# Routing search of a mixture of experts: four guessed rounds, the rest in a conditional on VectorE

## Chip, cores and metric

The kernel runs on one NeuronCore of a Trainium2 chip. The metric is the device time of one execution in microseconds; 630.14 us is the median of three runs before the change.

## What is computed

Attention with a sliding window, then a mixture of experts whose tokens are assigned greedily. In short:

```python
# q, k, v: (8, 8, 576, 64); window 64
x = softmax_window(q @ k.T / 8) @ v          # as 4608 tokens x 512
logits = x @ w_gate                          # 4608 x 8
cap = 4608 // 8                              # 576 tokens an expert
for idx in argsort(-logits.flatten()):       # best pair first
    tok, e = divmod(idx, 8)
    if assigned[tok] < 0 and counts[e] < cap:
        assigned[tok] = e; counts[e] += 1
out[mask_e] = relu(x[mask_e] @ w1[e]) @ w2[e]   # w1: 512x1024, w2: 1024x512
```

The greedy order needs no sort. Whichever expert fills first has the highest threshold: the score of its 576th token. The kernel finds that expert and its threshold, gives away all pairs above it, takes the expert out, and repeats for the next. Experts are numbered here in the order in which they fill, 0 to 7.

## The kernel before

The attention takes the first quarter of the time. It also leaves the scores in SBUF, as 128 partitions x 36 columns x 8 experts. Then two things run together for each of the eight experts: routing (finding the expert, its threshold and the list of its tokens) and the products.

**The search** (`search`) finds the threshold of an expert in eight rounds of four bits. A round compares each token's best score with 15 thresholds (`compare`, line 586, VectorE), counts the hits of every expert with nine matmuls (line 632, TensorE; the one-hot tile `one4` is the weight), and some thirteen short VectorE instructions find the highest threshold at which any expert is still full (lines 641 to 694). The next round's thresholds depend on it. Expert 0 is searched otherwise (`first`): three rounds in steps of the mean top score `mu`, and a conditional (line 765) with `search` as its block, on TensorE and VectorE, which is skipped when the three rounds have decided. Expert 7 takes what is left.

**Behind the search** come, in `steps`: the expert's number `ei` (line 946), which the loads of its weights read; its mark on every token, `X`; a scan (829); two matmuls for positions (832, 833); the listing of its 576 tokens (`listing`; 18 matmuls on 921, eight on 933, the index tile `idx` on 939); and the bookkeeping for the next search. Then `turn` gathers the tokens (line 1103, five indirect DMAs from GpSimd) and transposes them on TensorE (1141).

**The products** (`Experts.steps`): layer one is 160 matmuls (line 1203) over eight groups of 128 hidden units, layer two 112 (1237 and 1247). Every operand is split into a high and a low half in a faster float format. Weights come in chunks of 512 KB: SyncE loads `st`, ScalarE copies it to the high half and its negative to the low half, and a DMA from GpSimd adds `st` (line 1046) once the expert's gathers are issued. Eight chunks fit, which is one expert. VectorE subtracts low halves of the activations in layer one (1164, 1172) and adds once early in layer two (1224).

**Order.** The instructions of every engine are issued in an order fixed when the program is built. `Streams` is a small planner: generators yield the time that they think a step takes, and are resumed in order of planned time. So TensorE's queue holds products with the matmuls of search rounds, positions, lists and transposes put in at planned places, and waits in order at each. `yield lambda: ...` holds a generator until the condition is true in the plan; `self.dve(dt)` and `self.busy(dt)` book planned time on an engine. `ex.first` counts the layers one that are issued. In the kernel before, routing of the next expert starts as soon as that of the one before is finished, wherever the products are.

The loop that drives it:

```python
def route():
    for p in range(E):
        for dt in rt.steps(p):
            if p in rt.eint and p not in known and (p or rt.T is not None):
                known.add(p)
                st.add(ex.load(p, rt.eint[p]))
            yield dt
```

Of the kernel before, what the change touches and what calls it, by code (L numbers as in the profile page):

```python
# [10 lines left out]
FT = mybir.dt.float32  # L11
# [12 lines left out]
E = 8  # L24
# [415 lines left out]
BRANCH = [mybir.EngineType.PE, mybir.EngineType.DVE]  # L440
SLACK = (0, 0) + (100,) * 6
# [3 lines left out]
class Routing:  # L445
# [39 lines left out]
    def constants(self, jp, t):  # L485
# [20 lines left out]

        diag = t("diag", [128, 4])
# [70 lines left out]
    def mean_out(self):  # L578

        nc = self.nc  # L580
        nc.vector.tensor_scalar(self.mu, self.total, 1.0 / (128 * HEAD), None, op0=OP.mult)
        return [lambda: nc.vector.tensor_scalar(self.thr0, self.thr0, self.mu, None, op0=OP.mult)] + [lambda j=j: self.compare(self.G0, self.thr0, j, j + 4) for j in range(0, LATE, 4)]
# [25 lines left out]
    def search(self, p, code, one4, copied=0):  # L608

        nc, tile_ = self.nc, self.wk.tile  # L610
        slack = SLACK[p]
# [4 lines left out]
        for r in range(NR):  # L616
            G = tile_([128, NJ, ND], BF, name="G")
            c4 = self.room(128, 72)
            cn, c4 = c4[:, 64:72], c4[:, 0:4 * ND]
            for j0, j1 in ((0, 20), (20, 36)):  # L620
                self.compare(G, thr, j0, j1)
                yield self.dve(480 - 4 * j0)
            for f in rest:
                f()
            if r:
                self.dve(360, 2)
            yield max(slack, copied - self.clock() if not r else 0)
            kept, self.kept = self.kept, None
            if kept is not None:
                nc.tensor.matmul(cn, self.ones, kept, start=True, stop=True)  # L630
            for j in range(0, NJ, 4):
                nc.tensor.matmul(c4, one4[:, j // 4].rearrange("p k e -> p (k e)"),  # L632
                                 G[:, j:j + 4].rearrange("p j d -> p (j d)"),
                                 start=(j == 0), stop=(j == NJ - 4))
            self.joined()
            yield self.busy(350) + 200 + slack
            if kept is not None:
                nc.vector.tensor_tensor(self.left, self.left, cn, OP.add)

            dg = tile_([128, 4, ND], FT, name="dg")  # L640
            nc.vector.tensor_tensor(dg, c4.rearrange("p (k d) -> p k d", k=4),
                                    self.diag[:, :, None].to_broadcast([128, 4, ND]), OP.mult)
            sq = self.sq[r % 2]
            nc.vector.tensor_reduce(sq[:, 0:ND], dg.rearrange("p k d -> p d k"), axis=AX.X, op=OP.add)
            yield self.dve(530, 2) + (150 if kept is not None else 0)
            st = self.st
            nc.vector.transpose(st[:, 0:4].rearrange("p k e -> p (k e)"), sq)
            cnt = tile_([128, E], FT, name="cnt")
            nc.vector.tensor_reduce(cnt, st.rearrange("d k e -> d e k"), axis=AX.X, op=OP.add)
            yield self.dve(490, 2)  # L650

            step = float(1 << 28 - 4 * r) if r else 1.0
            pq = self.pq[r % 2]
            nc.vector.tensor_scalar(pq[:, 0:E], cnt, 0.0, step, op0=OP.is_ge, op1=OP.mult)
            pt = tile_([128, 32], FT, name="pt")
            nc.vector.transpose(pt, pq)
            yield self.dve(440, 2)
            ps = tile_([128, 1], FT, name="ps")
            nc.vector.tensor_reduce(ps, pt[:, 0:ND], axis=AX.X, op=OP.add)
            num = tile_([128, 32], FT, name="num")  # L660
# [61 lines left out]
    def first(self, code, X, run):  # L722
# [42 lines left out]
        with self.tc.If(go != 1):  # L765
# [3 lines left out]
            for _ in self.search(0, code, one4):  # L769
                pass  # L770
# [579 lines left out]
```

## Time and profile before

| | |
|---|---|
| three runs | 628.88, 630.14, 632.12 us |
| profiled execution | 627.58 us |
| its span, first to last instruction | 625.9 us |
| mean granted TensorE clock | 0.987 |
| TensorE busy | 598.2 us, 96% |
| VectorE busy | 457.8 us, 73% |
| ScalarE busy | 371.7 us, 59% |
| GpSimd busy | 187.2 us, 30% |

The profiled execution is a run of its own, with its own time beside its span; rows and stretches of the profile belong to it, not to the median. A busy share is the union of the times in which an engine had an instruction of the program in work. TensorE's matmuls are pipelined and overlap, so what one costs is read from the distance between starts, not from its duration.

### The profile page before, as it was taken

How to read it: one execution, taken by the hardware profiler on the slowest of the kernel's cores; microseconds unless marked ns; L12 is line 12 of the kernel's file. 1: busy time of each engine (PE TensorE's matmuls, PEld its weight loads, DVE VectorE, ACT ScalarE, POOL GpSimd, SP SyncE). 2: the span in 40 equal slices, each digit the busy share in tenths (PEclk: the TensorE clock that was granted, in tenths of full speed). 3: DMA queues.
4: the chain of work that ended last, by engine and by line, in shares of the span. 5: the costliest groups of instructions: out<-in, count | busy, mean ns of one | idle time of the engine just before them, and what ended most of it. 6: DMA issues, size and time to landing. Idle time of an engine off the chain costs nothing.

```text
span 625.9 us, 16201 instructions
## 1 busy us (share of the span) xinstructions
PE 598.2 (96%) x5966; PEld 509.8 (81%) x5966; DVE 457.8 (73%) x2151; ACT 371.7 (59%) x798; POOL 187.2 (30%) x245
## 2 busy tenths in 40 slices
PE   8999999996499999999999999999999999999996
PEld 6677778785399789888988988898889779888984
DVE  7888888887789779869977996898788717604400
ACT  6799889995474386267445837565564637515310
POOL 1324454440331261053126205321620560011011
PEclk9999999998699999999999999999999999999999
DMA  8999999951597599199659918975974798110001
GB/s 311 356 360 367 367 392 366 338 210 70 179 249 154 179 248 250 22 315 248 120 183 245 246 43 286 242 137 208 210 204 102 261 248 296 63 42 35 2 25 50
DMA packets 44944, 128.81 MB, mean 206 GB/s; under 512 B 4672, under 2 KB 5312, under 8 KB 44864
## 3 DMA queue, kind: packets, MB, share of 16 engines
q1 hardware_dynamic: 30592, 79.00, 35.2%
q0 software_dynamic: 13984, 48.25, 33.2%
q8 instruction: 47, 0.77, 0.5%
q10 hardware_dynamic: 288, 0.52, 0.3%
q14 instruction: 33, 0.27, 0.1%
HBM read 82.14 MB, written 18.87 MB: 161 GB/s over the span
## 4 chain that ended last, share of the span: by engine, by line
PE 53%; issue 17%; POOL 2%; DMA 1%; DVE 1%; ACT 1%; POOLq 0%; ACTq 0%
PE h L1203 24%; PE o L1247 20%; PE o L1237 3%; PE rps L632 2%; PE tp L1141 2%; POOL out L1226 2%; DMA xg<-xs,idx 1%; PE rps L593 1%; PE rps L921 1%; DMA xs<-x 0%; ACT R L905 0%; PE rps L923 0%; POOLq L1346 0%; DVE hl L1172 0%; PE rps L933 0%
## 5 line engine op out<-in xcount | busy, mean ns | idle before, releaser
L1203 PE MATMUL h<-xh,wh 128*128 128x320 f32 (+2 forms) x800 | 161.6, 333 | 0.0
L1203 PEld LDWEIGHTS h<-xh,wh 128*128 128x128 f32 x800 | 124.6, 188 | 5.2 <-ACT xh L1091 0.2
L1226 POOL DMA_INDIRECT out<-ot,idx x40 | 41.1, 1028 | 224.0 <-DVE ot L1224 79.6
L1247 PE MATMUL o<-wh,hl 128*128 128x512 f32 x256 | 101.0, 395 | 0.0
L1247 PE MATMUL o<-wl,hh 128*128 128x512 f32 x256 | 100.8, 394 | 0.0
L1247 PE MATMUL o<-wh,hh 128*128 128x512 f32 x256 | 100.7, 393 | 0.0
L141 ACT ACTIVATE pe<-st,mx 128x128 f32<-128x128 f32 x288 | 91.9, 393 | 5.7 <-DVE mx L136 5.5
L1203 PE MATMUL h<-xh,wl 128*128 128x256 f32 (+1 forms) x512 | 91.2, 297 | 0.0
L1203 PEld LDWEIGHTS h<-xh,wl 128*128 128x128 f32 x512 | 78.8, 188 | 4.4
L1030 ACT ACTIVATE wh<-st 128x1024 fp32r<-128x1024 f32 x64 | 67.3, 1051 | 2.8 <-DMA st<-w 2.8
L136 DVE CUSTOM_DVE_ANT_0 st<-Sp,mask 128x128 f32<-128x128 f32 x288 | 63.8, 285 | 6.7 <-PE Sp L128 5.7
L1217 ACT ACTIVATE ot<-o 128x512 f32<-128x512 f32 x32 | 19.1, 598 | 81.9 <-PE o L1247 81.8
L1046 POOL DMA_DIRECT2D wl<-st x51 | 46.5, 972 | 63.2 <-ACT wl L1044 34.2
L1247 PEld LDWEIGHTS o<-wh,hh 128*128 128x128 f32 x256 | 48.1, 188 | 9.5
L1247 PEld LDWEIGHTS o<-wl,hh 128*128 128x128 f32 x256 | 48.1, 188 | 9.4
L1247 PEld LDWEIGHTS o<-wh,hl 128*128 128x128 f32 x256 | 48.1, 188 | 9.3
L1044 ACT ACTIVATE wl<-wh 128x1024 fp32r<-128x1024 f32 x51 | 53.9, 1057 | 0.7
L1164 DVE TENSOR_TENSOR sum<-h,sum 128x256 f32<-128x256 f32 x56 | 23.2, 414 | 38.6 <-ACT sum L1162 38.4
L1167 ACT ACTIVATE hh<-h 128x320 fp32r<-128x320 f32 (+1 forms) x72 | 31.0, 431 | 31.1 <-PE h L1203 30.3
L150 ACT ACTIVATE pt<-Tp 128x512 f32<-128x512 f32 x72 | 42.1, 587 | 7.2 <-PE Tp L148 7.0
L1103 POOL DMA_INDIRECT xg<-xs,idx x32 | 31.2, 976 | 48.2 <-DVE eq L845 39.8
L176 PE MATMUL Op<-VO,pt 128*64 128x73 f32 x608 | 43.0, 230 | 1.0 <-issue 0.5
(210 smaller groups left out, 1100.4 us busy)
## 6 DMA issues: line engine op xcount, KB each, us to landing
st<-w SPq DMA_DIRECT2D x59, 512.0 KB, 7.3
wl<-st POOLq DMA_DIRECT2D x51, 512.0 KB, 6.4
xs<-x SPq DMA_DIRECT2D x36, 256.0 KB, 4.7
VO<-v SPq DMA_DIRECT2D x6, 1168.0 KB, 17.9
Q<-q SPq DMA_DIRECT2D x6, 1152.0 KB, 13.5
K<-k SPq DMA_DIRECT2D x6, 1152.0 KB, 16.1
VT<-vt SPq DMA_DIRECT2D x6, 1152.0 KB, 16.4
st<-w POOLq DMA_DIRECT2D x5, 512.0 KB, 7.5
```

What stands on the lines that cost most here:

```text
L136: nc.vector.tensor_tensor_reduce(st[:, h, :], Sp[h % 2][:, h // 2], mk, scale=-0.125, scalar=3.0e38, op0=OP.add, op1=OP.min, accum_out=mx[ ...
L141: nc.scalar.activation(pe[:, h, :], st[:, h, :], AF.Exp, bias=mx[:, h:h + 1], scale=-1.0)
L150: return pt, lambda: nc.scalar.activation(pt.rearrange("p h q -> p (h q)"), Tp, AF.Copy)
L176: nc.tensor.matmul(Op[g][64 * a:64 * a + 64, h, :], pt[:, h, 64 * a:64 * a + 64], vv[a][:, 4 * g + h, :], start=True, stop=True)
L1030: nc.scalar.activation(hi, st[i], AF.Copy)
L1044: nc.scalar.activation(lo, hi.bitcast(FT), AF.Copy, scale=-1.0)
L1046: nc.gpsimd.dma_start(lo.bitcast(FT), st[i], accum_op=OP.add)
L1103: nc.gpsimd.indirect_dma_start(out=g[a][0:n], out_offset=None, in_=self.xs, in_offset=IndirectOffsetOnAxis(ap=idx[0:n, a:a + 1], axis=0))
L1167: nc.scalar.activation(hh[:, f, c0:c1], h, AF.Relu)
L1203: nc.tensor.matmul(h[:, 0:w], wv[:, cc, 128 * (f % 2):128 * (f % 2) + 128], x[:, cc, x0:x0 + w], start=(k == 0), stop=(k == 4 * len(terms) ...
L1226: nc.gpsimd.indirect_dma_start(out=self.out[5 * p + a], out_offset=IndirectOffsetOnAxis(ap=idx[0:m, a:a + 1], axis=0), in_=ot[0:m], in_off ...
L1247: nc.tensor.matmul(o, ht[:, f, 128 * a:128 * a + 128], wt[:, 512 * (f % 2):512 * (f % 2) + 512], start=(k == 0), stop=(k == 23))
```

## The change

For experts 1 to 6 the search of eight rounds gives way to `guessed`: four rounds, with 15 thresholds each, that start from the threshold `T` of the preceding expert and cover the stretch from `T - 1.25 mu` to `T`; each round divides a sixteenth of the one before, the last in fifteen steps. The thresholds are floats from a table `gtab`, made in the setup by four instructions and scaled by `mu` once. The last round also counts whether one token more would fit, and writes into `go` the number of experts that fill there, or 0 if the step holds more than one token.

Then the stream is held until layer one of the preceding expert is issued (`opened`) and 700 planned ns more. A conditional on VectorE alone follows: if `go` is not 1, its block makes the whole search of eight rounds, with the counting done by VectorE products and sums (`alone`) in place of matmuls. The plan books 6000 + 300 ns for it. The number, the loads, the list and the gathers follow as before.

`search` is cut into `tally` (its old lines from the allocation of `c4` to `cnt`, moved as they are, and left out below), `alone` and `highest` (its old lines from `step` to `num`). Expert 0's search keeps its form; both conditionals now have the block named as not the preferred way on (`preferred_fallthrough_block=False`), and the plan's clocks are restored after the block.

```diff
 GUESS = 22
 LATE = 20
 BRANCH = [mybir.EngineType.PE, mybir.EngineType.DVE]
+ALONE = [mybir.EngineType.DVE]
+NG = 4
+WIDE = 1.25
 SLACK = (0, 0) + (100,) * 6
 U32 = mybir.dt.uint32
 
...
+        steps = t("gtab", [128, NG, ND])
+        for r in range(NG):
+            f, o = (WIDE / 16 ** (r + 1), 0.0) if r < NG - 1 else (WIDE / (ND * 16 ** r), -WIDE / (ND * 16 ** r))
+            yield nc.vector.tensor_scalar(steps[:, r], dgf, f, o, op0=OP.mult, op1=OP.add)
...
-    def search(self, p, code, one4, copied=0):
+    def tally(self, G, one4, r, rest, copied, slack):
...
+    def alone(self, G, r, rest):
+
+        nc, tile_ = self.nc, self.wk.tile
+        for f in rest:
+            f()
+        if not r:
+            self.P = tile_([128, E, 32], FT, name="P", bufs=1)
+            self.four = tile_([128, 5, E], FT, name="four", bufs=1)
+            nc.vector.memset(self.P, 0.0)
+            nc.vector.tensor_copy(self.four[:, 4], self.left)
+        P, four = self.P, self.four
+        Pt = tile_([128, E, 32], FT, name="Pt", bufs=1)
+        for e in range(0, E, 2):
+            H = tile_([128, NJ // 4, 4, 4 * E], BF, name="one4").rearrange("p q k e -> p (q k e)")
+            H = H[:, 0:2 * NJ * ND].rearrange("p (e j d) -> p e j d", e=2, d=ND)
+            nc.vector.tensor_tensor(H, G[:, None].to_broadcast([128, 2, NJ, ND]),
+                                    self.one[:, :, e:e + 2].rearrange("p j e -> p e j")[:, :, :, None]
+                                    .to_broadcast([128, 2, NJ, ND]), OP.mult)
+            nc.vector.tensor_reduce(P[:, e:e + 2, 0:ND], H.rearrange("p e j d -> p e d j"), axis=AX.X, op=OP.add)
+        nc.vector.transpose(Pt.rearrange("p e d -> p (e d)"), P.rearrange("p e d -> p (e d)"))
+        nc.vector.tensor_reduce(four[:, 0], Pt, axis=AX.X, op=OP.add)
+        for q in range(1, 4):
+            nc.vector.tensor_copy(four[0:32, q], four[32 * q:32 * q + 32, 0])
+        cnt = tile_([128, E], FT, name="cnt")
+        nc.vector.tensor_reduce(cnt[0:32], four[0:32].rearrange("d k e -> d e k"), axis=AX.X, op=OP.add)
+        for q in range(1, 4):
+            nc.vector.tensor_copy(cnt[32 * q:32 * q + 32], cnt[0:32])
+        yield 0
+        return cnt
+
+    def highest(self, cnt, r, step, n=1):
+
+        nc, tile_ = self.nc, self.wk.tile
+        pq = self.pq[r % 2]
+        for i in range(n):
+            nc.vector.tensor_scalar(pq[:, E * i:E * i + E], cnt, float(i), step, op0=OP.is_ge, op1=OP.mult)
+        pt = tile_([128, 32], FT, name="pt")
+        nc.vector.transpose(pt, pq)
+        yield self.dve(330 + 110 * n, 1 + n)
+        ps = tile_([128, 1], FT, name="ps")
+        nc.vector.tensor_reduce(ps, pt[:, 0:ND], axis=AX.X, op=OP.add)
+        num = tile_([128, 32], FT, name="num")
+        nc.vector.transpose(num, ps.to_broadcast([128, 32]))
+        yield self.dve(430, 2)
+        return num[:, 0:E * n]
+
+    def search(self, p, code, T, one4=None):
...
+            self.compare(G, thr, 0, NJ)
+            cnt = yield from self.alone(G, r, rest) if one4 is None else self.tally(G, one4, r, rest, 0, 0)
+            num = yield from self.highest(cnt, r, float(1 << 28 - 4 * r) if r else 1.0)
...
-                b2 = self.Tb if not p and r == NR - 1 else tile_([128, 1], I32, name="base")
+                b2 = T.bitcast(I32) if r == NR - 1 else tile_([128, 1], I32, name="base")
...
+    def guessed(self, p, code, one4, copied):
+
+        nc, tile_ = self.nc, self.wk.tile
+        tab, slack = self.gtab, SLACK[p]
+        if p == 1:
+            nc.vector.tensor_scalar(tab, tab, self.mu, None, op0=OP.mult)
+        base = tile_([128, 1], FT, name="base")
+        nc.vector.scalar_tensor_tensor(base, self.mu, -WIDE, self.T, op0=OP.mult, op1=OP.add)
+        thr = tile_([128, ND], FT, name="thr")
+        nc.vector.tensor_scalar(thr, tab[:, 0], base, None, op0=OP.add)
+        self.dve(450, 2)
+        rest = []
+        for r in range(NG):
+            G = tile_([128, NJ, ND], BF, name="G")
+            for j0, j1 in ((0, 20), (20, 36)):
+                self.compare(G, thr, j0, j1)
+                yield self.dve(480 - 4 * j0)
+            cnt = yield from self.tally(G, one4, r, rest, copied, slack)
+            if r == NG - 1:
+                break
+            num = yield from self.highest(cnt, r, tab[:, r, 0:1])
+            d = tile_([128, 1], FT, name="d")
+            nc.vector.tensor_reduce(d, num, axis=AX.X, op=OP.max)
+            thr = tile_([128, ND], FT, name="thr")
+            nc.vector.scalar_tensor_tensor(thr, tab[:, r + 1], d, base.to_broadcast([128, ND]), op0=OP.add, op1=OP.add)
+            b2 = tile_([128, 1], FT, name="base")
+
+            def rebase(b2=b2, base=base, d=d):
+                nc.vector.tensor_tensor(b2, base, d, OP.add)
+
+            rest = [rebase]
+            base = b2
+            yield self.dve(450, 2)
+        num = yield from self.highest(cnt, r, 1.0, 2)
+        d = tile_([128, 2], FT, name="d0", bufs=1)
+        nc.vector.tensor_reduce(d, num.rearrange("p (k e) -> p k e", k=2), axis=AX.X, op=OP.max)
+        q8 = tile_([128, E], FT, name="q8")
+        nc.vector.scalar_tensor_tensor(q8, num[:, 0:E], d[:, 0:1], self.all8, op0=OP.is_equal, op1=OP.mult,
+                                       accum_out=self.num1)
+        nc.vector.scalar_tensor_tensor(self.go, d[:, 0:1], d[:, 1:2], self.num1, op0=OP.is_gt, op1=OP.mult)
+        T = tile_([128, 1], FT, name="T")
+        oh = tile_([128, ND], FT, name="oh0", bufs=1)
+        nc.vector.scalar_tensor_tensor(oh, self.dgf, d[:, 0:1], thr, op0=OP.is_equal, op1=OP.mult, accum_out=T)
+        self.number(q8, code)
+        yield self.dve(1100, 5)
+        yield lambda: self.opened(p)
+        yield 700
+        go = nc.values_load(self.go[0:1, 0:1], engines=ALONE, min_val=0, max_val=E)
+        ends = dict(self.ends)
+        with self.tc.If(go != 1, preferred_fallthrough_block=False):
+            for _ in self.search(p, code, T):
+                pass
+        self.ends.clear()
+        self.ends.update(ends)
+        self.T = T
+        yield self.dve(6000) + 300
 
...
         go = nc.values_load(self.go[0:1, 0:1], engines=BRANCH, min_val=0, max_val=E)
         ends = dict(self.ends)
-        with self.tc.If(go != 1):
+        with self.tc.If(go != 1, preferred_fallthrough_block=False):
             one4 = tile_([128, NJ // 4, 4, 4 * E], BF, name="one4")
             nc.vector.tensor_copy(one4, one.rearrange("p (q k) e -> p q (k e)", k=4)[:, :, None, :]
                                   .to_broadcast([128, NJ // 4, 4, 4 * E]))
-            for _ in self.search(0, code, one4):
+            self.T = self.Tb.bitcast(FT)
+            for _ in self.search(0, code, self.T, one4):
                 pass
             self.marked(self.T, code, X, run)
+        self.ends.clear()
         self.ends.update(ends)
-        self.T = self.Tb.bitcast(FT)
         yield 0
 
     def steps(self, p):
@@ -794,7 +893,7 @@
                     nc.scalar.copy(one4[:, j0:j1], one1[:, j0:j1, None, :].to_broadcast([128, 3, 4, 4 * E]))
                 copied = self.clock() + self.busy(1260, "act") + 200
             if p:
-                yield from self.search(p, code, one4, copied)
+                yield from self.guessed(p, code, one4, copied)
             else:
                 run = tile_([128, 2 * NJ], BF, name="run")
                 self.expert(p, code, False)
@@ -1326,6 +1425,7 @@
             st.add(ex.turn(p, idx))
 
         known = set()
+        rt.opened = lambda p: ex.first >= p
         rt.listed, rt.spawn, rt.clock, rt.ends = listed, st.add, ex.clock, st.end
         st.add(route())
         st.add(products())
```

## Rows read from the trace of the kernel before

**Rows 1.** The page, part 1: busy time, share of the span, instructions.

```profile
PE 598.2 (96%) x5966; PEld 509.8 (81%) x5966; DVE 457.8 (73%) x2151; ACT 371.7 (59%) x798; POOL 187.2 (30%) x245
```

**Rows 2.** Waits of TensorE, 170 to 550 us: total, times, longest in us.

```profile
PE rps L921 <- POOL R L897: 0.8, 1, 0.8
PE tp L1141 <- DVE xh L1095: 0.3, 1, 0.3
```

**Rows 3.** TensorE's busy time, clock and DMA in a layer one.

```profile
231.00:258.00 27.00, 27.00 (x213) 1.00 0.78 176
```

**Rows 4.** Timeline of TensorE, early in layer two of expert 1.

```profile
260.01 0.39 PE L1237 MATMUL o<-wh,hh 128*128 128x512 f32 x1
...
260.82 0.39 PE L1237 MATMUL o<-wh,hh 128*128 128x512 f32 x1
```

**Rows 5.** Lines 1203, 1237 and 632 by windows: experts 1, 4, 6.

```profile
L1203 PE MATMUL h<-xh,wh x96: 302/309/482, 230.4 to 257.4; 128*128 128x320 f32 x64, 128*128 128x512 f32 x32
...
L1237 PE MATMUL o<-wh,hh x8: 388/389/393, 258.2 to 261.7; 128*128 128x512 f32 x8
...
L1203 PE MATMUL h<-xh,wh x96: 302/309/482, 401.3 to 427.6; 128*128 128x320 f32 x64, 128*128 128x512 f32 x32
...
L1237 PE MATMUL o<-wh,hh x6: 389/391/397, 428.4 to 430.8; 128*128 128x512 f32 x6
...
L632 PE MATMUL rps<-G,one x54: 188/191/202, 399.0 to 422.9; 128*128 128x60 bf16 x54
...
L1203 PE MATMUL h<-xh,wh x96: 302/309/398, 515.9 to 540.4; 128*128 128x320 f32 x64, 128*128 128x512 f32 x32
...
L1237 PE MATMUL o<-wh,hh x5: 389/393/397, 541.1 to 543.7; 128*128 128x512 f32 x5
```

**Rows 6.** Timeline of VectorE and TensorE at expert 0's conditional.

```profile
158.11 0.31 DVE L720 TENSOR_TENSOR_SCAN run<-X 128x72 bf16<-128x72 bf16 x1
...
159.41 0.22 PE L832 MATMUL h<-X,tri 128*128 128x72 bf16 x1 [3.09 <-DVEq L765]
```

**Rows 7.** Timeline of VectorE, from the end of expert 1's layer one.

```profile
259.18 0.21 DVE L1172 SCALAR_TENSOR_TENSOR hh<-h,hh 128x64 fp32r<-128x64 f32 x1
...
263.01 0.68 DVE L1224 TENSOR_TENSOR ot<-o,low 64x512 f32<-64x512 f32 x1 [0.19 <-ACT low L1221]
...
264.14 0.14 DVE L946 TENSOR_SCALAR ei<-code 1x1 int32<-1x1 f32 x1
...
265.48 0.31 DVE L829 TENSOR_TENSOR_SCAN run<-X 128x72 bf16<-128x72 bf16 x1
```

**Rows 8.** The chain that ended last: start us, us, what.

```profile
200.94 0.93 PE o L1237 x4
201.87 0.27 PE rps L632 x9
...
210.99 0.05 PE rps L832
...
215.27 0.54 PE rps L921 x18
...
485.36 3.20 PE o L1237 x14
488.55 0.54 PE rps L921 x18
```

**Rows 9.** Line 1141, 200 to 232 us: idle before it, times.

```profile
  DMA xg<-xs,idx: 0.5, 2
```

**Rows 10.** Line 1046, 223 to 223.5 us: ns, start, time to landing.

```profile
L1046 POOL DMA_DIRECT2D wl<-st x1: 1021/1021/1021, 223.2 to 223.2; - x1
...
DMA to landing us min/median/max: 5.5/5.5/5.5
```

**Rows 11.** The page, part 6: KB each, median us to landing.

```profile
st<-w SPq DMA_DIRECT2D x59, 512.0 KB, 7.3
```

**Rows 12.** Groups of VectorE, 204 to 262 us: busy us, mean ns, idle.

```profile
L908 DVE TENSOR_TENSOR B<-r,sb 128x1152 bf16<-128x1152 bf16 x1 | 1.3, 1266 | 0.0
```

More of the change, by code (lines that the diff above doesn't have):

```diff
@@ L606, in dve @@
         return self.busy(dt - 110 * n, "dve") + 110 * n
-    def search(self, p, code, one4, copied=0):
+    def tally(self, G, one4, r, rest, copied, slack):
         nc, tile_ = self.nc, self.wk.tile
-        slack = SLACK[p]
+        c4 = self.room(128, 72)
+        cn, c4 = c4[:, 64:72], c4[:, 0:4 * ND]
+        for f in rest:
+            f()
+        if r:
+            self.dve(360, 2)
+        yield max(slack, copied - self.clock() if not r else 0)
+        kept, self.kept = self.kept, None
+        if kept is not None:
+            nc.tensor.matmul(cn, self.ones, kept, start=True, stop=True)
+        for j in range(0, NJ, 4):
+            nc.tensor.matmul(c4, one4[:, j // 4].rearrange("p k e -> p (k e)"),
+                             G[:, j:j + 4].rearrange("p j d -> p (j d)"),
+                             start=(j == 0), stop=(j == NJ - 4))
+        self.joined()
+        yield self.busy(350) + 200 + slack
+        if kept is not None:
+            nc.vector.tensor_tensor(self.left, self.left, cn, OP.add)
+        dg = tile_([128, 4, ND], FT, name="dg")
+        nc.vector.tensor_tensor(dg, c4.rearrange("p (k d) -> p k d", k=4),
+                                self.diag[:, :, None].to_broadcast([128, 4, ND]), OP.mult)
+        sq = self.sq[r % 2]
+        nc.vector.tensor_reduce(sq[:, 0:ND], dg.rearrange("p k d -> p d k"), axis=AX.X, op=OP.add)
+        yield self.dve(530, 2) + (150 if kept is not None else 0)
+        st = self.st
+        nc.vector.transpose(st[:, 0:4].rearrange("p k e -> p (k e)"), sq)
+        cnt = tile_([128, E], FT, name="cnt")
+        nc.vector.tensor_reduce(cnt, st.rearrange("d k e -> d e k"), axis=AX.X, op=OP.add)
+        yield self.dve(490, 2)
+        return cnt
@@ new lines, in alone @@
+    def alone(self, G, r, rest):
+        nc, tile_ = self.nc, self.wk.tile
+        for f in rest:
+            f()
+        if not r:
[16 more added lines that the diff above has]
+            nc.vector.tensor_copy(four[0:32, q], four[32 * q:32 * q + 32, 0])
+        cnt = tile_([128, E], FT, name="cnt")
+        nc.vector.tensor_reduce(cnt[0:32], four[0:32].rearrange("d k e -> d e k"), axis=AX.X, op=OP.add)
+        for q in range(1, 4):
+            nc.vector.tensor_copy(cnt[32 * q:32 * q + 32], cnt[0:32])
+        yield 0
+        return cnt
@@ L617, in search @@
             G = tile_([128, NJ, ND], BF, name="G")
[L618 to L659, printed above, removed]
@@ L691, in search, with first @@
             q2 = tile_([128, E], FT, name="q8")
-            def highest(q2=q2, num=num, d=d, q8=q8):
+            def first(q2=q2, num=num, d=d, q8=q8):
                 nc.vector.scalar_tensor_tensor(q2, num, d[:, 0:1], q8, op0=OP.is_equal, op1=OP.mult)
-            rest.append(highest)
+            rest.append(first)
             q8 = q2
-            yield self.dve(450, 2) if r else self.dve(700, 3)
         for f in rest:
             f()
-        yield self.dve(450, 2)
-        self.T = base.bitcast(FT)
@@ L703, in search @@
         self.number(q8, code)
+    def guessed(self, p, code, one4, copied):
+        nc, tile_ = self.nc, self.wk.tile
+        tab, slack = self.gtab, SLACK[p]
[49 more added lines that the diff above has]
+        yield self.dve(6000) + 300
```

6 lines of the change are left out of this document (1 added, 5 removed).

## Prediction

> **What bounds the kernel now.** I read the page's share of each engine first: TensorE is busy 96% of the span [rows 1]. A busy TensorE can still hide waits, so the next view is what its matmuls waited for from 170 us, where the first expert's products begin, to 550 us: two waits, 1.1 us in all, neither of them in a search [rows 2]. The reader is to see that nothing holds TensorE there. Its clock doesn't either: in a layer one with search rounds the granted clock is 1.00, the 2.4 GHz level, and TensorE busy for all of 27 us [rows 3]. So the experts are one queue of matmuls, and what a search costs is the place of its own matmuls in that queue. By the program there are eight rounds of nine counting matmuls (line 632) for each of experts 1 to 6: 48 rounds, 432 matmuls. A microsecond of them taken out is a microsecond off the end, as long as what replaces them comes in time.
>
> **What a round costs TensorE.** There are three readings. The chain gives a round 0.27 us, from the first of its matmuls to the next product's [rows 8]. The timeline gives more: from 260.01 to 260.82 stand two products of layer two and a round, and products alone follow each other in 0.23 us (four in 0.93 us, rows 8), so the round is 0.81 - 0.46 = 0.35 us [rows 4]; the product behind it is late as well. Whole layers give the third: layer one of expert 4 begins at 401.3 and layer two at 428.4, 27.1 us, with five rounds inside (six in the window, the first at 399.0 ahead of the layer); that of expert 6, with none, runs from 515.9 to 541.1, 25.2 us [rows 5]; 1.9 / 5 = 0.38 us. I take the middle one, 0.35, which is read directly and with all that belongs to the round; the ends are 0.27 and 0.38.
>
> **What the change removes.** Four of eight rounds for six experts: 24 rounds, 24 x 0.35 = 8.4 us of TensorE (6.5 to 9.1). Four rounds of VectorE work leave each layer one too, over a dozen short instructions each. Since TensorE waits for none of it now [rows 2], that gives nothing.
>
> **What it adds.** (a) Four table instructions in the setup. Short VectorE instructions take 0.14 to 0.21 us [rows 7], so between 0, if they fall into gaps of the attention, and 0.8 us; between such ends I take 0.4. (b) The guessed rounds do what the old ones did, in floating point for bits: nothing. The last has one more comparison and five short instructions after it, some 1.2 us at 0.2 each; then the stream waits for layer two, about a third of a layer later, and this hides it. Without that wait the listing would come 1.2 us later.
>
> (c) Six conditionals on VectorE. The trace has one, that of expert 0, and its skip can be read: VectorE's last instruction before it ends at 158.42, and TensorE's first matmul behind it, released by line 765, starts at 159.41 [rows 6]. So a skip is at most 0.99 us, the hand-over to TensorE included. The new ones are issued 0.7 us into layer two. For expert 2, layer two of expert 1 begins at 258.2 [rows 5]; VectorE's last instruction for layer one ends at 259.39 and its next duty to the products, the addition on line 1224, starts at 263.01 [rows 7]. The skip stands between, with 3.6 us of cover: nothing. Behind it on VectorE wait that addition and the expert's number, X and scan, and for these the position matmuls. The program puts those 0.7 + 6.3 + 0.78 + 0.65 + 0.44 = 8.9 us into layer two (its own planned steps). From the number's start, 264.14, to the scan's end, 265.79, VectorE needs 1.65 us, the addition 0.7. With 1.2 us until VectorE is free, a skip up to 8.9 - 1.2 - 0.7 - 1.65 = 5.3 us (a hand-over included) holds up nothing; every microsecond beyond is TensorE's, six times.
>
> (d) The moved step. An expert's number, weights, listing and gathers now begin in layer two of the preceding expert, however early the search ended. This passes SyncE's queue (the loads read the number) and GpSimd's (five gathers, then the low halves of the weights). The listing's matmuls came 4.3 us behind the position matmuls (210.99 to 215.27), so they will stand 13.2 us into layer two. Before, that was 14.3 us for expert 1 (200.94 to 215.27) and had drifted to 3.2 us for expert 6 (485.36 to 488.55) [rows 8]. So expert 1 gains a microsecond, expert 6 loses ten, and expert 1's rows show what the late place costs: its transposes waited 0.5 us for gathered rows [rows 9], and its first low half, issued behind the gathers at 223.2, landed 5.5 us later at 228.7 [rows 10], while layer one began at 230.4 [rows 5] and wants it after four products, at 231.3. That left 2.6 us. The new place is 1.1 us earlier and layer two shorter by two rounds, 0.7 us, so about 3 us are left. The cost is 0 to 0.5 us each for experts 2 to 6; I take 0.2, in all 1.0 us, being nearer to hidden. If the cover were gone, each microsecond of delay would be TensorE's.
>
> (e) Expert 0's block goes out of the straight path. By rows 6 this can save up to 0.99 us; if the new path is worse it can lose as much: 0.
>
> A rule speaks against (c). The Trainium skill (Runtime: NRT & Kernel Launch, section Instruction fetch mechanics) says that instructions stream in sequentially and that a taken branch to a place not yet loaded stalls for a fetch. The one skip of this trace took 0.99 us at most [rows 6], so here it shows no stall as long as a transfer of rows 11. What a stall would make of the time is the second rival below.
>
> **The sum.** -8.4 + 0.4 + 1.0 = -7.0 us. The profiled execution took 627.58 us (span 625.9), so the changed one would show 620.6. The median of the runs, 630.14, is 2.56 above the profiled one: 623.1 us is the forecast.
>
> **The rivals.** *Late weights or rows.* The late place bites harder than it did for expert 1. If the first low half takes 4 us more than the 5.5 us of rows 10, the 3 us are used up and layer one waits 1 us, in six experts 6 us: 623.1 + 6 = 629.1 us. For it: later experts' transfers share the queues with the preceding expert's stores, and a weight load from memory takes 7.3 us in the median [rows 11]. Against: TensorE waited for no weights at expert 1's place [rows 2].
>
> *The skip is long* (slower). VectorE has to fetch the code it jumps to, and does nothing until it is there. No row times that. The ends are nothing beyond the 0.99 us of rows 6 and a whole weight load, 7.3 us [rows 11]; then a skip is 8.3 us, 3.0 over the 5.3, and six cost 18 us: 641 us. The gain is gone where a skip takes 5.3 + 7.0 / 6 = 6.5 us. For it: the new blocks hold eight rounds of over twenty-five instructions, more than expert 0's. Against: rows 6, the nearest in kind.
>
> *The guess misses*, its block runs, and the change doesn't do what it says. On VectorE alone a round counts by four products over 1080 elements and four sums of as many; at the 1.27 us of the row with 1152 elements [rows 12] that is at least 8 x 1.2 = 9.6 us, eight rounds 77 us, nearly all in the open: about 700 us for one miss. Against: worked out from the reference's inputs, each of the six thresholds lies 0.002 to 0.84 mean scores under the one before (the window is 1.25), and the next score is 0.0005 or more below, against a finest step of 0.00002.
>
> **How the numbers follow.** The forecast case gets 0.78, late weights 0.12 (0.05 of it, with half the delay, still faster by over 0.5%), the long skip 0.08, a miss 0.02. A measurement of this kernel tells about 0.5%, 3.2 us, from no change; its three runs lie 3.2 us apart. So faster 0.83, same 0.07, slower 0.10. Low end: rounds at 9.1, expert 0's skip at 0.99 and the two additions at nothing give 620.0; with a microsecond for the spread of runs, 619.0. High end: the smallest saving, 6.5, with 0.8 and 2.5 added gives 626.9; 627.5 takes in the near part of the late weights.
>
> **What would show it.** The counting matmuls should number 216 instead of 432. Layer one of expert 4 should take some 26.4 us instead of 27.1 (three rounds inside instead of five), the period of an expert 1.4 us less. Position matmuls should stand about 8.9 us into layer two, listing 13.2, with no wait of TensorE in front. VectorE should show a hole of about a microsecond early in layer two and none of the block's work. The forecast is wrong if that hole passes 5.3 us, if a layer one begins with a wait for weights or transposes, or if a layer one doesn't shrink by 0.35 us for each round it lost.

## The result and the profile after

Four runs of the changed kernel took 619.33 to 622.03 us, median 620.21; four of the kernel before 628.88 to 632.12, median 630.78. The ratio is 0.984 (95% interval 0.980 to 0.987): faster by 10.6 us where 7.0 were forecast, and inside the range. The two profiled executions, 627.58 and 619.33 us, differ by 8.25.

The page of the changed kernel, its first part, answers to [rows 1]: VectorE lost 60 us of work and 319 instructions, TensorE 216 instructions, the counting matmuls of 24 rounds, as said.

```profile
PE 591.4 (96%) x5750; PEld 505.6 (82%) x5750; DVE 397.6 (64%) x1832; ACT 372.8 (60%) x798; POOL 186.2 (30%) x245
```

What TensorE waited for from 165 to 550 us (total, times, longest in us) answers to [rows 2]. The wait for the listing (0.8 us) is gone. The first row is new: four times TensorE now waits for VectorE's comparisons ahead of a counting round.

```profile
PE rps L629 <- DVE G L593: 1.3, 4, 0.3
PE tp L1240 <- issue: 0.5, 1, 0.5
PE tp L1240 <- DVE xh L1194: 0.2, 1, 0.2
PE h L1302 <- DVE xh L1194: 0.2, 1, 0.2
```

Layers one and two of experts 4 and 6, by windows of lines 1302, 1336 and 629 (xcount: duration min/median/max in ns, first and last start in us), answer to [rows 5].

```profile
L1302 PE MATMUL h<-xh,wh x96: 303/309/483, 394.4 to 421.1; 128*128 128x320 f32 x64, 128*128 128x512 f32 x32
...
L1336 PE MATMUL o<-wh,hh x8: 389/389/398, 421.9 to 425.1; 128*128 128x512 f32 x8
...
L629 PE MATMUL rps<-G,one x27: 188/191/202, 395.5 to 406.9; 128*128 128x60 bf16 x27
...
L1302 PE MATMUL h<-xh,wh x96: 302/309/471, 507.0 to 532.0; 128*128 128x320 f32 x64, 128*128 128x512 f32 x32
...
L1336 PE MATMUL o<-wh,hh x1: 394/394/394, 532.7 to 532.7; 128*128 128x512 f32 x1
```

Three rounds (27 matmuls) stand in expert 4's layer one now, not five, and yet it takes 27.5 us (394.4 to 421.9), where [rows 5] gave 27.1 and the prediction 26.4: one of its own signs of being wrong came true. The period of an expert shrank by 1.0 us on average, not 1.4. TensorE's timeline at its start shows why (start, us, what, the idle time before it in brackets):

```profile
394.26 0.33 PE L1240 MATMUL tp<-identr,xg 128*128 128x128 f32 x2
394.43 0.70 PE L1302 MATMUL h<-xh,wh 128*128 128x512 f32 x2
395.46 0.59 PE L629 MATMUL rps<-G,one 128*128 128x60 bf16 x9 [0.33 <-DVE G L593]
395.88 0.72 PE L1302 MATMUL h<-xh,wh 128*128 128x512 f32 x2
...
397.62 0.45 PE L1240 MATMUL tp<-identr,rest 128*128 128x128 f32 x4
```

From the first product to the one behind the round are 1.45 us. Two products take 0.46 and a round 0.35, so 0.64 us are lost to the wait, about twice the idle time that the row names. Experts 2, 3 and 5 have such a row too (0.31 to 0.34 us). The four transposes at 397.62 are the other new guest: in the kernel before, this expert's transposes ended in layer two of the one before it. They cost a layer one about 0.45 us (expert 6: 25.7 against 25.2 us, with no round in either) and the layer two they left gains as much.

The moved step stands where it was forecast, and without a wait. TensorE's timeline and the chain of the changed kernel, layer two of expert 1 beginning at 254.6: position matmuls 9.6 us into it (8.9 said), listing 14.0 (13.2 said).

```profile
264.14 0.21 PE L931 MATMUL rps<-X,tri 128*128 128x72 bf16 x1
...
268.57 0.54 PE rps L1020 x18
```

The same stretch on VectorE, which answers to [rows 7]:

```profile
255.60 0.21 DVE L1271 SCALAR_TENSOR_TENSOR hh<-h,hh 128x64 fp32r<-128x64 f32 x1
259.07 0.68 DVE L1323 TENSOR_TENSOR ot<-o,low 64x512 f32<-64x512 f32 x1 [3.26 <-ACT low L1320]
259.68 0.13 DVE L1045 TENSOR_SCALAR ei<-code 1x1 int32<-1x1 f32 x1
...
261.05 0.31 DVE L928 TENSOR_TENSOR_SCAN run<-X 128x72 bf16<-128x72 bf16 x1
```

The skip lies in the 3.26 us of idle time in the second row, which ends because ScalarE delivers `low`, not because the skip is over. So this row doesn't tell how long the skip is. (An 8 KB packet on the second instruction queue begins 1.3 to 1.5 us into the gap, here at 257.28, and likewise for the other five experts; the run with less time booked, below, shows what a skip with such a packet takes.) The scan ends at 261.36, 2.8 us before TensorE reaches the position matmuls.

Expert 0's conditional, which answers to [rows 6]: from the scan's end, 158.06, to the first matmul behind are 0.52 us, where it was 0.99.

```profile
157.75 0.31 DVE L818 TENSOR_TENSOR_SCAN run<-X 128x72 bf16<-128x72 bf16 x1
...
158.58 0.22 PE L931 MATMUL h<-X,tri 128*128 128x72 bf16 x1 [2.62 <-DVEq L863]
```

**Where the 8.45 us came from**, by the starts of the layers, summed over the experts up to the layer one of expert 7: 1.26 us before expert 0's layer one, 0.57 in the layers one, 6.6 in the layers two. Ahead of the first of these the kernels differ by the setup and the form of one block, yet it is not a steady point: layer one of expert 0 begins at 170.53 us in this execution of the changed kernel and at 172.91 in another one further down, while that of before has 171.79. Ahead of it TensorE idles on the routing of expert 0, and its granted clock is at or near the 1.2 GHz level (0.50 from 150 to 165 us in the profile after; 0.61, then 0.50 in that of before). So experiments are compared by the *stretch* from the start of expert 1's layer one to that of expert 7's, read from TensorE's timelines. It holds 39 rounds before and 19 after:

| kernel | from | to | stretch, us |
|---|---|---|---|
| before | 230.39 | 568.85 | 338.46 |
| after | 227.95 | 560.41 | 332.46 |

### The profile page after: what moved, and what is told of

The parts are those of the page before. It is cut to its first block, busy times and chain, and to the rows that moved or that the text cites. A ratio compares the mean times of both kernels' runs of the same rounds, so it can differ in the third digit from the quotient of the medians.

```text
span 617.4 us, 15509 instructions
## 1 busy us (share of the span) xinstructions
PE 591.4 (96%) x5750; PEld 505.6 (82%) x5750; DVE 397.6 (64%) x1832; ACT 372.8 (60%) x798; POOL 186.2 (30%) x245
## 4 chain that ended last, share of the span: by engine, by line
PE 49%; issue 17%; DVE 4%; POOL 4%; DMA 1%; ACT 1%; POOLq 0%; DVEq 0%
PE h L1302 25%; PE o L1346 18%; PE o L1336 4%; POOL out L1325 2%; PE rps L629 1%; DVE xh L1194 1%; PE tp L1240 1%; POOL xg L1202 1%; POOL wl L1145 1%; DMA xg<-xs,idx 1%; PE rps L1020 1%; ACT xh L1190 0%; DMA xs<-x 0%; DVE G L593 0%; POOL rest L1202 0%
## 5 line engine op out<-in xcount | busy, mean ns | idle before, releaser
L1302 PE MATMUL h<-xh,wl 128*128 128x256 f32 (+1 forms) x512 | 89.7, 296 | 0.0
L1266 ACT ACTIVATE hh<-h 128x320 fp32r<-128x320 f32 (+1 forms) x72 | 30.8, 428 | 30.9 <-PE h L1302 30.4
L1271 DVE SCALAR_TENSOR_TENSOR hl<-h,hh 128x256 fp32r<-128x256 f32 x72 | 30.3, 421 | 23.7 <-ACT hh L1266 23.5
```

The lines of the kernel that those rows point to most:

```text
L1266: nc.scalar.activation(hh[:, f, c0:c1], h, AF.Relu)
L1271: nc.vector.scalar_tensor_tensor(t, h[:, a - c0:b - c0], 0.0, hh[:, f, a:b].bitcast(FT), op0=OP.max, op1=OP.subtract)
L1302: nc.tensor.matmul(h[:, 0:w], wv[:, cc, 128 * (f % 2):128 * (f % 2) + 128], x[:, cc, x0:x0 + w], start=(k == 0), stop=(k == 4 * len(terms) ...
```

## The experiments

My theory was that of the prediction: a round costs what its nine matmuls displace in TensorE's queue, and the skips and the late place are covered. The rivals were that the lighter VectorE gives the gain, that expert 0's new form of block does, and that the skips eat part of it. Ratios are to runs of the kernel before on the same chip.

**Expert 0's block alone** (in the kernel before; the four table instructions stay out, and so does a clamp of `mu` at 0, a part of the change that the diff above doesn't show):

```diff
-        with self.tc.If(go != 1):
+        with self.tc.If(go != 1, preferred_fallthrough_block=False):
...
+        self.ends.clear()
         self.ends.update(ends)
```

> The kernel before with one part of the change alone: expert 0's block out of the straight path, and the plan's clocks restored behind it. Theory (the gain is the places of 24 rounds in TensorE's queue): only the start moves, by the 0.5 us that the skip shortened and what follows from it, so 0.5 to 1.3 us off the span of 625.9 us and layers as before. Rival (order: the gain comes from the plan's repaired clocks and the new form of the conditional): most of the 8.5 us, a span near 618 us.

Median 630.34 us against 630.14, ratio 1.001 (0.998 to 1.004). The hand-over did shrink, from 0.99 us to 0.51 (scan ended 159.42, matmul 159.93), but layer one of expert 0 began at 171.94, not 171.79. Whether the half microsecond reaches the end, runs that agree to 0.3% can't tell; that most of the gain comes from here is ruled out, and the rival falls.

**The counting matmuls twice** (the changed kernel; the second nine count the same again):

```diff
+        for again in range(2):
             for j in range(0, NJ, 4):
                 nc.tensor.matmul(c4, one4[:, j // 4]..., G[:, j:j + 4]..., ...)
-        yield self.busy(350) + 200 + slack
+        yield self.busy(620) + 200 + slack
```

> The changed kernel with the nine counting matmuls of each guessed round issued twice, the second set overwriting the first; VectorE's work is the same. Theory: 216 matmuls more at 0.03 us are 6.5 us on the 617.4 us span, about 624 us. Rival (VectorE's relief is the gain, TensorE's matmuls are hidden): 617 to 618 us. A new wait for the comparison at the start of layer one could swallow up to 0.27 us in four of the 24.

Median 630.16, ratio 1.001 (0.998 to 1.003): some 10 us above the changed kernel, more than the theory's figure. The stretch is 335.77, 3.3 us longer. Its layers two give the clean reading: those of experts 1 to 4 hold one doubled round each and took 28.54 to 28.59 us instead of 28.31 to 28.36, so nine matmuls more cost 0.23 us there, near the 0.27 of [rows 8]. Layers one of experts 2 to 5, with three doubled rounds, took about 0.6 us more, while the new wait in them shrank from 1.3 us in all to 0.5. The rest came ahead of the stretch: the layers of expert 0 took 33.0 us instead of 28.96 and 30.4 instead of 28.5, with this wait in the same view as above.

```profile
PE tp L1241 <- DMA rest<-xs,idx: 1.7, 1, 1.7
```

So TensorE's time in a round does count, but this experiment shifted expert 0's gathers as well and is a poor measure of its size.

**VectorE's work back**, after the guess and before the hold: four sets (`range(4)`), each a round's comparisons and three times the short instructions of `highest`; results unused.

```diff
         yield self.dve(1100, 5)
+        for again in range(4):
+            Gx = tile_([128, NJ, ND], BF, name="G")
+            for j0, j1 in ((0, 20), (20, 36)):
+                self.compare(Gx, thr, j0, j1)
+                yield self.dve(480 - 4 * j0)
+            yield 650
+            for n in range(3):
+                yield from self.highest(cnt, n, 1.0)
         yield lambda: self.opened(p)
```

> The changed kernel with VectorE's work of four more rounds behind each guessed search (comparison and the short instructions, 3.2 us each, results unused), without their matmuls. Theory: layer one has room on VectorE, so nothing, 617 to 618 us of span. Rival (VectorE's relief is the gain): most of the 8.5 us is lost again, 624 to 626 us.

Median 669.81, ratio 1.064 (1.060 to 1.069). That is 50 us, which neither side expected. The four sets didn't fit into layer one: the position matmuls came 16.8 us into layer two, not 9.6, and everything behind them was late. TensorE's waits (165 to 590 us) and its windows in three of the layers one (window, us, busy us and matmuls of PE, then PEld, DVE, ACT and POOL, clock, DMA share, GB/s):

```profile
PE tp L1248 <- DVE xh L1202: 8.0, 8, 2.6
PE tp L1248 <- DMA xg<-xs,idx: 7.2, 6, 2.7
```

```profile
236.00:246.00 10.00, 8.99 (x41) 7.26 (x42) 8.11 (x31) 5.93 (x10) 3.81 (x5) 0.52 1.04 213
300.00:310.00 10.00, 9.00 (x48) 7.55 (x49) 8.37 (x31) 6.07 (x12) 3.58 (x4) 0.66 1.04 213
363.00:373.00 10.00, 9.08 (x42) 7.49 (x43) 7.99 (x30) 5.29 (x9) 3.54 (x4) 0.55 1.04 213
```

The waits for rows and transposes are 15 us. The clock is a further part: around the start of a layer one the granted clock was 0.52 to 0.66 behind these waits, at or near the 1.2 GHz level. The two were not added up to the 50 us. The run measured the edge of the late place's cover, not VectorE's load, so it was repeated with half the work:

```diff
-        for again in range(4):
+        for again in range(2):
```

> As the variant with VectorE's work of four more rounds, but of two, which end within layer one of the preceding expert, so that the listing isn't pushed. Theory (VectorE's relief gives nothing, and what the four sets cost was the listing pushed 7 us into layer two): 332 to 333.5 us from layer one of expert 1 to that of expert 7. Rival (VectorE's load itself holds TensorE): half of the loss seen with four sets, 15 us or more.

Median 621.48, ratio 0.985 (0.979 to 0.991); beside it, on the same chip, the changed kernel itself:

> The changed kernel once more, for comparison on the same chip as its variants. Ratio to the kernel before 0.980 to 0.988. From layer one of expert 1 to layer one of expert 7 it took 332.5 us in its first profile against 338.5 us before; the start, up to expert 1, should vary by 1 to 2 us from run to run, this stretch by less than 0.5 us.

621.50, 0.985 (0.979 to 0.991). The stretches are 332.85 and 331.83; the 1.0 us between them is layer one of expert 1 (27.68 against 26.64 us), where the sets made a counting round wait for its comparisons. Two rounds' VectorE work per search costs nothing that the medians show, and VectorE's load as the main source of the gain falls. All four rounds' work can't be put back within the cover, so its full load is not tested.

**Without the conditionals of experts 1 to 6** (the guess is taken as it is):

```diff
-        go = nc.values_load(self.go[0:1, 0:1], engines=ALONE, min_val=0, max_val=E)
-        ends = dict(self.ends)
-        with self.tc.If(go != 1, preferred_fallthrough_block=False):
-            for _ in self.search(p, code, T):
-                pass
-        self.ends.clear()
-        self.ends.update(ends)
```

> The changed kernel without the six conditionals and their blocks: the guess is taken as it is; the hold until layer two and the planned 6.3 us stay. Theory: the skips are hidden in VectorE's hole early in layer two, so within 0.5 us of 617.4 us. Rival (the skips cost part of the gain): 1 us or more faster.

Median 622.88, ratio 0.990 (0.988 to 0.993), and a stretch of 332.92 against 332.46: the skips cost nothing here. The profiled execution is 2.8 us above that of the changed kernel, nearly all of it from ahead of the stretch: expert 0's layer one began 1.2 us later and its two layers took 1.4 us more.

**A skip in the open.** With less time booked for the block, the number comes earlier and the skip no longer hides behind `low`.

```diff
-        yield self.dve(6000) + 300
+        yield self.dve(1500) + 300
```

> The changed kernel with 1500 planned ns for the skip in place of 6000, so that the position matmuls stand 4.4 us into layer two and the number and X go ahead of the addition on VectorE. Theory (a skip of about 1 us, and a late place that costs nothing): no wait at the position matmuls, listing 4.5 us earlier, the stretch from expert 1 to 7 within 1.5 us of 332.5 us. Rival (a skip of 3 us, which the idle stretch of VectorE from 255.81 to 259.07 us would also allow): TensorE waits 1.5 to 2 us for X in each of six experts, the stretch at 340 us or more.

Median 626.03, ratio 0.992 (0.990 to 0.996), stretch 333.35. The listing stands 9 to 10 us into layer two, not 14, and the kernel is no faster. TensorE's waits (165 to 550 us):

```profile
PE rps L931 <- DVE X L913: 1.8, 3, 0.8
PE rps L1020 <- POOL R L996: 1.2, 1, 1.2
```

The wait for comparisons at the start of layers one is gone in this order, so old and new waits about cancel, and the stretch alone doesn't price the place of the listing. VectorE's timeline shows the skips of experts 2 and 3:

```profile
257.10 0.21 DVE L1271 SCALAR_TENSOR_TENSOR hh<-h,hh 128x64 fp32r<-128x64 f32 x1
258.17 0.14 DVE L1045 TENSOR_SCALAR ei<-code 1x1 int32<-1x1 f32 x1 [0.86 <-DVEq L795]
...
312.22 0.21 DVE L1271 SCALAR_TENSOR_TENSOR hh<-h,hh 128x64 fp32r<-128x64 f32 x1
315.60 0.14 DVE L1045 TENSOR_SCALAR ei<-code 1x1 int32<-1x1 f32 x1 [3.16 <-issue]
```

One skip takes 0.86 us (those of experts 5 and 6 0.87 and 0.86), the next 3.16 (expert 4's 3.17), with nothing that VectorE waits for. In those two long gaps the trace has an 8 KB packet on the second instruction queue (at 313.8 and 370.1 us), and in the short one at 258 none. Behind expert 5's short skip VectorE stood still for another 1.60 us four instructions later, beside a packet at 426.7. The run's median is 4.5 us above that of the changed kernel, while the profiled execution, the lowest of its ten runs at 622.52, is only 1.05 above; where the rest goes has no trace.

**The second guessed round later** takes away the new wait: the round is planned 900 ns later, so that its comparisons are there.

```diff
-        yield max(slack, copied - self.clock() if not r else 0)
+        yield max(slack, copied - self.clock() if not r else 0) + (900 if r == 1 else 0)
```

> The changed kernel with the second guessed round planned 900 ns later. In the changed kernel's profile four of these rounds stand 0.4 us into layer one and wait 0.65 us for the comparison on line 593. Theory (that wait is lost time, made by the place alone): it goes, 2.0 to 2.6 us less in the stretch from expert 1 to 7, 330 to 330.5 us. Rival (TensorE would wait somewhere else for the same VectorE work): 332.5 us.

Median 619.76, ratio 0.983 (0.977 to 0.989), stretch 330.33, and no wait for a comparison is left. Layers one of experts 2, 4 and 5 take 26.8 us where they took 27.4; that of expert 3 takes 27.2, with a product that starts 0.3 us late for no reason that the profile shows. Run again on another chip:

> The variant with four rounds and the second one later, once more beside the one with three: 330 to 330.5 us in the stretch; median 1 to 2.6 us under the changed kernel's 621.5 us of the last comparison.

619.54, 0.985 (0.982 to 0.988), stretch 330.30. The stretch repeats to 0.03 us and is 2.1 below that of after (1.5 below the changed kernel's second execution, where each wait was 0.17 us, not 0.33). The median moves by less than it can tell.

**Three rounds**, with the later second one. The last step is 0.0003 mean scores, still under the 0.0005 to the next score in these inputs; in inputs with closer scores the block would run.

```diff
-NG = 4
+NG = 3
```

> Three guessed rounds in place of four (the finest step is then 0.00033 mean scores, still below the smallest distance of 0.0005 in these inputs), with the second round planned 900 ns later. Theory (0.35 us a round): six rounds less than the variant with four and the later place, of which five lie between layer one of expert 1 and that of expert 7: 330.3 - 1.75 = 328.6 us there, the median 2.1 us below that variant's 619.8 us. Rival (the rounds left are hidden, nothing more to gain): 330 us there.

Median 615.05 (614.48 to 617.07), ratio 0.978 (0.976 to 0.981), the best of all. The stretch, 328.16, is 2.14 shorter than that of the run before for five rounds less: 0.43 us a round. But 0.68 of it is layer one of expert 3, where the late product of the run before is gone too; the other four lost 0.33 to 0.40 us each, the 0.35 of the prediction. The median fell by 4.5 us, so more than half of that lies ahead of the stretch or isn't explained.

**Without the hold** and with the small booking, so that routing runs ahead again:

```diff
-        yield lambda: self.opened(p)
-        yield 700
...
-        yield self.dve(6000) + 300
+        yield self.dve(1500) + 300
```

> The changed kernel without the hold: the conditional stands right behind the guessed search, in layer one of the preceding expert, with 1500 planned ns. The variant with the hold and 1500 ns showed skips of 0.86 us, and 3.16 us for experts 3 and 4. Theory (the cover is VectorE's idle stretch in layer two; in layer one the evacuations queue behind the skip): a long skip is more than the three buffers of layer one's sums cover, so TensorE waits 0.5 to 1.5 us in the experts with a long skip, nothing in the others; the listing returns to its early place, which gives nothing: 331 to 335 us from layer one of expert 1 to that of expert 7. Rival (the late place costs, so the early one gains): under 330 us.

Median 635.37, ratio 1.008 (1.005 to 1.011), stretch 341.86: worse than before the change, against every expectation. TensorE's waits (165 to 560 us) and the worst place on VectorE:

```profile
PE rps L929 <- DVE X L911: 7.6, 4, 4.2
PE rps L1020 <- ACT R L1002: 2.9, 1, 2.9
```

```profile
274.66 0.08 DVE L804 DVE_READ_ACCUMULATOR2_ANT code<- 128x1 f32 x1
281.80 0.14 DVE L1043 TENSOR_SCALAR ei<-code 1x1 int32<-1x1 f32 x1 [7.05 <-issue]
```

VectorE stands still for 7 us at a conditional, waiting for nothing that the profile shows, and TensorE's position matmuls, put close behind it in the plan, wait 4.2 us; then the granted clock is 0.62 from 284 to 288 us. One 8 KB instruction packet lies in the 7.05 us, and it begins 5.2 us into them, where it began 1.3 to 1.4 us into the long gaps of the run above. TensorE around its wait (window, us, busy us and matmuls of PE, clock, DMA share, GB/s):

```profile
279.00:284.00 5.00, 0.67 (x5) 0.96 0.37 98
284.00:288.00 4.00, 4.00 (x12) 0.62 0.76 250
```

Of the five gaps at this run's conditionals that no other wait hides, the shortest (1.0 us) has no packet. Those of 3.6 and 3.7 us have one, and ahead of it the DMA engines moved nothing (share 0.00); in those of 5.0 and 7.05 us the share ahead of it was 0.98 and 1.05. That a fetch which must queue behind other transfers makes the gap longer is therefore likely; no run tests it. Nor is it shown that the skips make up all of the 9.4 us by which the stretch exceeds that of after. But without the hold VectorE's gaps reach TensorE; with it they don't.

**One miss**, a single run: expert 3's block made to run, though its guess was good.

```diff
-        with self.tc.If(go != 1, preferred_fallthrough_block=False):
+        with self.tc.If(go != (9 if p == 3 else 1), preferred_fallthrough_block=False):
```

> The changed kernel with the conditional of expert 3 made to enter its block whatever the guess found, the other five as they are. One look. The prediction put a miss at 77 us or more, all but some 5 us of it in the open; with the reductions at the 0.67 us of 288 elements scaled to 1080, 2.5 us, a round is 19 us and the block 150 us. Theory: 70 to 150 us more in layer two of expert 2, and TensorE's clock at the lower level behind the wait.

759.36 us. TensorE's wait, and the two large groups of the block on VectorE (busy us, mean ns, idle):

```profile
PE o L1346 <- DVE ei L1045: 136.1, 1, 136.1
```

```profile
L668 DVE TENSOR_REDUCE P<-one 128x30 f32<-128x1080 bf16 x32 | 66.7, 2085 | 1.1
L665 DVE TENSOR_TENSOR one<-G,one 128x1080 bf16<-128x1080 bf16 x32 | 40.7, 1272 | 0.0
```

Layer two of expert 2 took 167.6 us instead of 28.4. So a miss costs 139 us, nearly all of it in the open, 13 times the gain of the change.

## Why the prediction was right, step by step

**The rounds (right, in kind and in size).** The whole change goes by TensorE's queue. Layers with a known number of rounds price one, if their starts are read to two decimals. For the kernel before, TensorE's timeline has these (starts of layers one and two of experts 4 and 6):

```profile
401.34 0.63 PE L1203 MATMUL h<-xh,wh 128*128 128x512 f32 x2
...
428.38 0.39 PE L1237 MATMUL o<-wh,hh 128*128 128x512 f32 x1
...
515.85 0.61 PE L1203 MATMUL h<-xh,wh 128*128 128x512 f32 x2
...
541.12 0.39 PE L1237 MATMUL o<-wh,hh 128*128 128x512 f32 x1
```

| layer one | rounds in it | four transposes in it | us |
|---|---|---|---|
| before, expert 4 | 5 | no | 27.04 |
| before, expert 6 | 0 | no | 25.27 |
| second round later, expert 4 | 3 | yes | 26.78 |
| three rounds, expert 4 | 2 | yes | 26.42 |
| after, expert 6 | 0 | yes | 25.71 |

The first two give 1.77 / 5 = 0.35 us a round, the others 1.07 / 3 and 0.71 / 2, 0.36 each. The prediction's third reading, 0.38, is the first of these with starts rounded to 0.1 us. So the reading that it chose was right, and 24 rounds are 8.5 us instead of 8.4. In the stretch 20 rounds left, 7.1 us; the old wait for the listing, 0.8, went as well; the new wait took 2.6 back (0.64 in each of four layers one). That makes 5.3 of the 6.0 us measured. The 0.7 left are not explained; about half of them lie in layer two of expert 3.

**"Nothing" for the guessed rounds, (b) (wrong, by 2.6 us in this execution).** The instructions cost nothing, but their place did. "The guessed rounds do what the old ones did" left out that a search now starts at another moment: its second round falls 0.5 us into layer one with its comparisons not ready. A wait that [rows 2] doesn't have was put in by the new order; planning that round 0.9 us later took it out, and the stretch became 2.1 us shorter. This is also why "layer one of expert 4, 26.4 us" failed: 27.1 - 0.7 for two rounds + 0.65 for the wait + 0.45 for transposes = 27.5, as measured.

**The late place, (d) (cost overstated).** 1.0 us was put down for five places. In the profile after no transposes of experts 2 to 6 waited for rows and no layer one for weights, so nothing that shows was lost. That the cover has an end is shown by the run with four sets of VectorE work, 7 us later: 50 us. The rival of late rows exists, but its place begins beyond the one chosen; no run's waits show late weights.

**The skips, (c) (right to call them covered, wrong on their length).** "At most 0.99 us" holds for the short ones, 0.86. Others take 3.16 us in this placement, within the 5.3 us of cover, and removing all six gained nothing in the stretch. The Trainium skill (Runtime: NRT & Kernel Launch, Instruction fetch mechanics) says that a taken branch out of the loaded window must fetch before it goes on. The trace agrees: the two gaps of 3.16 and 3.17 us have a packet of the instruction queue in them, the short ones none, and 3.16 - 0.86 puts the price at 2.3 us. It is argued, not shown, that the packet is VectorE's and that the skip is the taken branch; for the second speaks that in the run with the miss VectorE entered its block after 0.35 us of idle time. The rival's mechanism is therefore likely real. It lost by the cover; in the run without the hold, which had gaps of up to 7 us and waits of TensorE behind them, the kernel was slower than before, the side which that rival foretold.

**Setup and expert 0, (a) and (e).** Put at +0.4 and 0. Neither can be told: the shorter hand-over of 0.5 us is shown, its effect on the time isn't, since expert 0's layer one started 2.4 us apart in two executions of the changed kernel itself. The 1.26 us that this trace gained there is no part of the explanation.

**The miss.** "At least 77 us" was called a lower bound, and the sum that used it, about 700 us, was too low: 139 were measured, and 759.36 us in all. The sums over 1080 elements take 2.09 us, not the 1.2 scaled from a product of plain elements [rows 12]; the products measured 1.27.

So the sum, -7.0, met a difference of 8.25 us between the profiled executions, and that it came so near is in part luck. A wait of 2.6 us was not foreseen; on the other side the charges of 1.4 us for setup and late place did not show, the end of the listing's old wait (0.8) was not foreseen, and some 1.7 us, 0.7 in the stretch and 1.0 ahead of it, are not explained. The medians differ by more, 10.6 us here and 9.4 on another chip; what lies between them and the profiled executions has no trace.

## What to carry to other kernels

Where one engine's queue is full, cost a piece of work by the whole stretch with and without it, not by its own instructions, and then look at which moment each remaining piece now falls: a step that wasn't edited can arrive before its data. A branch that is nearly always skipped can be free if the work behind it is held to a place where nobody waits for that engine; measure the cover by pushing more work into it, and price the branch that isn't skipped.

## What the runs showed of the hardware

- A short wait of TensorE cost about 0.3 us more than the idle time in its row: 0.64 us between products where the row names 0.33, and 0.48 us of a layer one (27.26 against 26.78) where it names 0.17, in the second execution of the changed kernel.
- A skipped conditional on VectorE took 0.86 or 3.16 us in one execution, the long ones with an 8 KB instruction packet in the gap; in another order up to 7.05 us, with the DMA engines busy all the time (share 1.05) until the packet began.
- Waits of TensorE were followed by a lower granted clock: 0.62 for the 4 us behind the wait of 4.2 us, and 0.52 to 0.66 in the first 10 us of layers one behind waits for rows of 0.8 to 2.7 us.
- After the 136 us of idling in the run with the miss the granted clock was 0.52, near the 1.2 GHz level, from 457 to 463 us, and then 1.00:

```profile
457.00:463.00 6.00, 5.66 (x14) 4.12 (x15) 4.71 (x16) 1.54 (x2) 2.16 (x3) 0.52 0.62 192
463.00:470.00 7.00, 7.00 (x54) 5.43 (x53) 3.50 (x13) 4.54 (x6) 2.43 (x3) 1.00 0.98 379
```
